# The cosine half of a transformed product in three float32r passes, in the banks of the sine half

## The chip, the cores and the metric

One NeuronCore of a Trainium2 chip runs the whole program. The metric is device time in microseconds (us): how long one execution takes. Four compute engines matter: TensorE (PE, with PEld for its weight loads) multiplies matrices into PSUM, VectorE (DVE) and ScalarE (ACT) work elementwise and read PSUM, GpSimd (POOL) works elementwise in SBUF alone and starts gathers; the SP queue starts most transfers. Each engine runs its own instructions in program order, and semaphores hold one back until what it needs from another is done.

## The reference

```python
X = np.fft.fft(x, axis=1); X = np.fft.fft(X, axis=2)    # x: (8, 3008, 256)
x = X.real.astype(np.float32).reshape(24064, 256)
h = x @ w_in                                            # w_in: (256, 2048)
g = h * np.clip(h + 3.0, 0.0, 6.0) / 6.0
out = (g @ w_out).astype(np.float32)                    # w_out: (2048, 256)
```

The real part of a two-dimensional Fourier transform of each of 8 images, and on every row of it an MLP with one hidden layer of 2048 and a hard-swish.

## The kernel before

**The transform.** The sequence of 3008 is taken as 47 x 64. `stage1` does the transform over 47 for a pair of images, `stage2` the one over 64; the transform over the 256 columns is folded into w_in, so that a row's hidden value is a cosine part plus or minus a sine part. Two output rows, k1 and N1 - k1, share both parts: h+ = c + n + s and h- = c + n - s, where n comes from one more column (`qn` times the row `WN` of folded weights). So the MLP's first product is done once for two rows, in two halves: `W1[:, 0]` with `q[:, 0]` (cosine) and `W1[:, 1]` with `q[:, 1]` (sine).

**Steps.** The program is one list of 384 steps: 4 pairs of images (p), 12 chunks of 256 columns in a pair (ck; the last of a pair has 192, or 194 in the first product), and 8 parts of the hidden layer in a chunk (fc), each of 256 hidden values, done as two blocks i of 128. t = 8 ck + fc counts the steps of a pair. The first 8 steps (0 to 7) prepare the weights beside the work, steps 8 to 21 use plain float32 products for both halves, and from `SPLIT` = 22 on the order is the one that the change touches. That loop issues, in step s:

1. `odd_half` (L642) of step s + 2: the sine half. Its six products are float32r: q and w were split by `split_q` (L605) and `split_w` (L619) into a high part, a low part and a rest, so that three passes give the exact product: the rest's pass into bank v, then high and low into bank u, on top of the cosine half that stands there. ScalarE copies v to y (L653), VectorE adds u (1 + EPS) + y in u (L655), ScalarE does the relu of it to t (L692). Between the copy and the addition come the products of a stage1 (`begin_parts`), if one is due.
2. the first n of the seven products of `mlp2` (L743) of step s: w_out, by a Strassen-like scheme of seven products for eight, three with a (the gated values) and four with sums c of a.
3. `even_half` (L627) of step s + 3: the cosine half, float32, two products (L632) into bank u, which VectorE adds to qn times `WS1` as s (L638).
4. the products of a stage2, if one is due (`middle_fns`), which ScalarE evicts to q (L529 and L490).
5. VectorE's `other_sign` (v = u - 2 (1 + EPS) s, L663), its relu, the two gates to a (L695); GpSimd's `combine` to c (L697, its adds at L709) of step s + 1, and at the head of a chunk (fc 0) the five adds of `finish` (L755) for the chunk before; VectorE's transposes of its results (L804) at fc 1 and 2.
6. the remaining products of `mlp2` of step s. At fc 7 ScalarE evicts the finished sums to e (L753).

**Banks.** PSUM has eight banks here: four of the tag acc for the output sums, and a0, a1, y0, y1. Bank u of a step is a{step % 2} and v is y{step % 2}. A stage1 or stage2 in step s takes y{(s + 3) % 2} (`bank`), a stage1 also a{(s + 3) % 2} (`other_bank`):

```python
if turn_of[0]:
    return ps_u.tile(shape, F32, tag=f"y{turn_of[0] % 2}", name=name)   # turn_of[0] = s + 3
```

A tile with a tag waits until the readers of the tag's last tile are done.

**When.** A stage2 comes at t = 3 and 7 of every 16 (fc 3 and 7), in pair 0 partly at other steps; a stage1 every ninth step of pairs 1 and 2, every sixth of pair 0 from t = 32, none in pair 3.

Of the kernel before, what the change touches and what calls it, by code (L numbers as in the profile page):

```python
# [60 lines left out]
def kernel(  # L61
# [34 lines left out]
    DH = 32  # L96
# [37 lines left out]
    C = consts.tile([P, 2, D], F32, name="C")  # L134
    W1 = consts.tile([P, 2, FF], F32, name="W1")
    WN = consts.tile([P, NFC], F32, name="WN")
    WS1 = consts.tile([P, NFC], F32, name="WS1")
    G = consts.tile([P, 7, NF, P], F32, name="G")
    half = consts.tile([P, 1], F32, name="half")
    ones = consts.tile([P, P], F32, name="ones")  # L140
# [148 lines left out]
    def stage1(pr, c):  # L289
# [16 lines left out]
        nc.scalar.copy(z[:, 1], ps[1][0:PB + PZ])  # L306
        yield
        nc.scalar.copy(z[:, 0], ps[0][0:PB + PZ])
# [57 lines left out]
    def evict_first(hb, m, ps, pt):  # L366
        k = FIRST.index(m)
        pool, tag = ((zpool, "z"), (zpool, "z"), (apool, "a"), (cpool, "c"))[k]
        z = pool.tile([P, 2, 2, D + 1], F32, tag=tag, name="z")
# [22 lines left out]
    def stage1_quarters(hb, m):  # L392
# [14 lines left out]
        nc.scalar.copy(z[:, 1], ps[1][0:PX])  # L407
        yield
        nc.scalar.copy(z[:, 0], ps[0][0:PX])
# [171 lines left out]
    def activate(ch, fc, u, v, between=None):  # L581
        of, nq, qn = ch.ck % 2 * TB, ch.nq, ch.pr.qn[ch.ck // 2]
        wn, back = (WN, 1.0) if ch.ck < 2 else (WS1, 1.0 + EPS)
        s = spool.tile([P, 2, TB], F32, tag="s", name="s")
        for i in range(2):
            f = 2 * fc + i
            nc.vector.scalar_tensor_tensor(s[:, i, 0:nq], qn[:, of:of + nq], wn[:, f:f + 1], u[:, i, 0:nq],  # L587
                                           op0=AL.mult, op1=AL.add)
# [3 lines left out]
        t = spool.tile([P, 2, 2, TB], F32, tag="t", name="t")  # L592
        ch.a[fc] = a
        nc.vector.scalar_tensor_tensor(u[:], s[:], back, v[:], op0=AL.mult, op1=AL.add)
        relu(t[:, 0], u[:], 1.0 / 6.0)
        nc.vector.scalar_tensor_tensor(v[:], s[:], -back, v[:], op0=AL.mult, op1=AL.add)
# [8 lines left out]
    def split_q(ch):  # L605

        of, nq, q = ch.ck % 2 * TB, ch.nq, ch.pr.q[ch.ck // 2][:, 1]
        k = qpool.tile([P, 3, TB], F32R, tag="k", bufs=2, name="k")
        ch.k = k
        split(k[:, 0, 0:nq], k[:, 1, 0:nq], k[:, 2, 0:nq], q[:, of:of + nq])  # L610

    def split(high, low, rest, x):
        nc.scalar.mul(high, x, 1.0 - EPS / 2.0)
        h = high.bitcast(F32)
        nc.gpsimd.tensor_tensor(low, x, h, op=AL.subtract)
        nc.scalar.mul(rest, h, EPS)
        nc.gpsimd.tensor_tensor(rest, rest, low, op=AL.subtract)

    def split_w(i):  # L619

        cs = slice(i * TB, (i + 1) * TB)
        low, rest = (spool.tile([P, TB], F32, tag="part", name="part") for j in range(2))
        split(KW[:, 0, cs], low[:], rest[:], W1[:, 1, cs])
        nc.scalar.mul(KW[:, 1, cs], low[:], 1.0 / EPS)
        nc.scalar.mul(KW[:, 2, cs], rest[:], -1.0 / EPS)

    def even_half(ch, fc, step):  # L627
        of, nq, q = ch.ck % 2 * TB, ch.nq, ch.pr.q[ch.ck // 2]
        u = ps_u.tile([P, 2, TB], F32, tag=f"a{step % 2}", name="u")
        for i in range(2):  # L630
            f = 2 * fc + i
            nc.tensor.matmul(u[:, i, 0:nq], W1[:, 0, f * P:(f + 1) * P], q[:, 0, of:of + nq],  # L632
                             start=(i == 0), stop=True, skip_group_check=True)
        qn = ch.pr.qn[ch.ck // 2]
        s = spool.tile([P, 2, TB], F32, tag="s", name="s")
        for i in range(2):
            f = 2 * fc + i
            nc.vector.scalar_tensor_tensor(s[:, i, 0:nq], qn[:, of:of + nq], WS1[:, f:f + 1], u[:, i, 0:nq],  # L638
                                           op0=AL.mult, op1=AL.add)
        ch.front[fc] = [u, s]  # L640

    def odd_half(ch, fc, step, between):  # L642
        nq, (u, s) = ch.nq, ch.front[fc]
        v = ps_u.tile([P, 2, TB], F32, tag=f"y{step % 2}", name="v")
        for j, o in ((2, v), (0, u), (1, u)):
            for i in range(2):
                fs = slice((2 * fc + i) * P, (2 * fc + i + 1) * P)
                nc.tensor.matmul(o[:, i, 0:nq], KW[:, j, fs], ch.k[:, j, 0:nq],  # L648
                                 start=(j == 2 and i == 0), stop=True, skip_group_check=True)
        y = spool.tile([P, 2, TB], F32, tag="y", bufs=1, name="y")  # L650
        t = spool.tile([P, 2, 2, TB], F32, tag="t", name="t")
# [8 lines left out]
    def other_sign(ch, fc):  # L660
        nq, (u, v, t, s) = ch.nq, ch.front[fc]
        un, vn, sn, tn = u[:, :, 0:nq], v[:, :, 0:nq], s[:, :, 0:nq], t[:, :, :, 0:nq]
        nc.vector.scalar_tensor_tensor(vn, sn, -2.0 * (1.0 + EPS), un, op0=AL.mult, op1=AL.add)  # L663
# [49 lines left out]
    def mlp2_first(ch, fc, halves=(0, 1)):  # L713
        a = ch.a[fc]
        for h in halves:
# [5 lines left out]
            if fc == NF - 1:  # L721
                if h == 0:
                    ch.r = epool.tile([P, 2, 2, TB], F32, tag="r", bufs=1, name="r")
                for m in range(2):
                    nc.scalar.mul(ch.r[:, m, h], ch.acc[h][:, m], (1 - 2 * m) / WS)

    def mlp2(ch, fc, part=None, n=3):
# [11 lines left out]
        for i, mv in order:  # L739
# [5 lines left out]
            if fc == NF - 1 and (i % 2 == 1 or i == 6):  # L745
                if i == 1:
                    ch.e = epool.tile([P, 8, TB], F32, tag="e", bufs=1, name="e")
# [7 lines left out]
    def finish(ch):  # L755
# [3 lines left out]
        w = epool.tile([P, 3, TB], F32, tag="w", bufs=1, name="w")  # L759
        r = epool.tile([P, 2, 2, TB], F32, tag="r", bufs=1, name="r")  # L760
        wn, rn = w[:, :, 0:n], r[:, :, :, 0:n]
# [676 lines left out]
```

## Time and profile before

| | us |
|---|---|
| median of 3 runs (1880.35 to 1881.13) | 1880.74 |
| the profiled execution's own time | 1880.88 |
| its span | 1879.1 |
| VectorE busy | 1421.0 (76%) |
| ScalarE busy | 949.6 (51%) |
| GpSimd busy | 1523.3 (81%) |

The granted clock of TensorE was 0.998 of full speed. In a line of the timeline stand the start and the duration in us, the engine, the line of the program, the operation, out<-in by the program's names, the shape, and how many instructions were merged; in brackets is the idle time ahead of it and what ended that. A float32 product of 256 columns is two instructions, a float32r product one. The start of a TensorE instruction can lie a little before the one ahead of it has streamed out, so lengths are read between like instructions of successive steps. Groups show the busy time and the mean of one in ns.

### The profile page before, as it was taken

The numbers are of one execution on the slowest core, as the hardware profiler recorded it, in microseconds if no ns is written. First come the engines' busy times: TensorE is split into PE (matmuls) and PEld (weight loads), VectorE is DVE, ScalarE is ACT, GpSimd is POOL, SyncE is SP. The second block draws the span as 40 slices with busy tenths as digits, with TensorE's granted clock in tenths as the row PEclk, the third lists the DMA queues.
The fourth block names the chain that finished last, engine by engine and source line by source line (L and its number), as shares of the span: only waits on it lengthen the run. The fifth ranks groups of instructions, "written<-read, shape, count | busy, mean of one in ns | idle before, by whom it ended". The sixth has DMA issues, their size and how long they took to land.

```text
span 1879.1 us, 30498 instructions
## 1 busy us (share of the span) xinstructions
PE 1861.5 (99%) x10176; PEld 1639.5 (87%) x10176; DVE 1421.0 (76%) x2756; ACT 949.6 (51%) x1647; POOL 1523.3 (81%) x1764
## 2 busy tenths in 40 slices
PE   9999999999999999999999999999999999999998
PEld 6678888888998888888998888888899898999987
DVE  8966777777777777777787777777778777777777
ACT  6545454554554554544455545445454454445443
POOL 5698999997789888898778888889777777777775
PEclk9999999999999999999999999999999999999999
DMA  7432233421112222221112221222110111101001
GB/s 267 113 100 65 63 96 82 96 56 34 49 40 60 69 69 74 53 55 44 38 49 58 58 68 51 57 64 56 48 40 21 40 28 27 42 19 40 19 22 21
DMA packets 157380, 110.42 MB, mean 59 GB/s; under 512 B 122095, under 2 KB 135898, under 8 KB 157222
## 3 DMA queue, kind: packets, MB, share of 16 engines
q1 hardware_dynamic: 144966, 71.24, 15.1%
q0 software_dynamic: 11008, 36.63, 6.7%
q8 instruction: 81, 1.33, 0.3%
q10 hardware_dynamic: 1248, 0.59, 0.1%
q14 instruction: 77, 0.63, 0.1%
HBM read 71.93 MB, written 36.79 MB: 58 GB/s over the span
## 4 chain that ended last, share of the span: by engine, by line
PE 91%; DVE 3%; POOL 2%; issue 1%; ACT 1%; DMA 1%; SPq 0%; DVEq 0%; POOLq 0%; ACTq 0%
PE acc L743 57%; PE u L632 16%; PE u L648 9%; PE v L648 4%; PE ps L526 2%; PE ps L296 1%; POOL c L709 1%; DVE a L695 1%; PE v L577 1%; PE acc L719 1%; ACT t L692 1%; PE u L577 1%; POOL xt L188 0%; DVE top L882 0%; DVE s L587 0%
## 5 line engine op out<-in xcount | busy, mean ns | idle before, releaser
L743 PE MATMUL acc<-c,G 128*128 128x256 f32 (+1 forms) x3008 | 698.6, 375 | 0.4 <-POOL c L709 0.2
L743 PEld LDWEIGHTS acc<-c,G 128*128 128x128 f32 x3008 | 564.4, 190 | 76.1 <-POOL c L709 4.5
L709 POOL TENSOR_TENSOR c<-a 128x512 f32<-128x512 f32 (+1 forms) x375 | 470.8, 1255 | 193.8 <-DVE a L695 165.6
L743 PE MATMUL acc<-a,G 128*128 128x256 f32 (+1 forms) x2256 | 599.7, 376 | 0.0
L692 ACT ACTIVATE t<-v,half 128x512 f32<-128x512 f32 (+1 forms) x384 | 261.0, 680 | 356.4 <-DVE v L663 355.0
L743 PEld LDWEIGHTS acc<-a,G 128*128 128x128 f32 x2256 | 395.2, 190 | 52.3 <-issue 14.3
L638 DVE SCALAR_TENSOR_TENSOR s<-qn,WS,u 128x256 f32<-128x256 f32 (+1 forms) x720 | 309.4, 471 | 162.2 <-PE u L632 161.2
L692 ACT ACTIVATE t<-u,half 128x512 f32<-128x512 f32 (+1 forms) x384 | 260.8, 679 | 300.1 <-DVE u L655 262.3
L655 DVE SCALAR_TENSOR_TENSOR u<-u,y 128x512 f32<-128x512 f32 (+1 forms) x360 | 245.4, 682 | 193.6 <-ACT y L653 190.5
L632 PE MATMUL u<-q,W 128*128 128x256 f32 (+1 forms) x1440 | 362.8, 374 | 0.0
L695 DVE SCALAR_TENSOR_TENSOR a<-t,v 128x512 f32<-128x512 f32 (+1 forms) x480 | 265.7, 570 | 57.3 <-ACT t L692 54.9
L632 PEld LDWEIGHTS u<-q,W 128*128 128x128 f32 x1440 | 270.5, 190 | 34.6
L653 ACT COPY y<-v 128x512 f32<-128x512 f32 (+1 forms) x360 | 208.6, 580 | 174.4 <-PE v L648 172.7
L709 POOL TENSOR_TENSOR c<-a,c 128x256 f32<-128x256 f32 (+1 forms) x375 | 269.5, 719 | 29.4
L709 POOL TENSOR_TENSOR c<-c,a 128x256 f32<-128x256 f32 (+1 forms) x375 | 269.5, 719 | 29.4
L695 DVE SCALAR_TENSOR_TENSOR a<-t,u 128x512 f32<-128x512 f32 (+2 forms) x448 | 261.0, 594 | 15.4 <-ACT t L692 15.4
L663 DVE SCALAR_TENSOR_TENSOR v<-s,u 128x512 f32<-128x512 f32 (+1 forms) x360 | 243.7, 677 | 0.9 <-ACT t L692 0.7
L648 PE MATMUL u<-k,KW 128*128 128x256 f32 (+1 forms) x1440 | 226.1, 279 | 0.0
L648 PE MATMUL v<-k,KW 128*128 128x256 f32 (+1 forms) x720 | 208.7, 371 | 0.0
L648 PEld LDWEIGHTS u<-k,KW 128*128 128x128 f32 x1440 | 193.7, 188 | 0.0
L648 PEld LDWEIGHTS v<-k,KW 128*128 128x128 f32 x720 | 136.0, 190 | 17.1
L709 POOL TENSOR_TENSOR r<-w,e 128x256 f32<-128x256 f32 (+1 forms) x92 | 88.9, 988 | 3.6
(152 smaller groups left out, 1228.9 us busy)
## 6 DMA issues: line engine op xcount, KB each, us to landing
out_dram<-o SPq DMA_DIRECT2D x744, 32.0 KB
T<-in_c_stage_dram SPq DMA_DIRECT2D x26, 512.0 KB
g<-zd SPq DMA_DIRECT2D x42, 256.0 KB
zd<-z SPq DMA_DIRECT2D x48, 192.0 KB
xt<-in_x_dram POOLq DMA_DIRECT2D x21, 256.0 KB
qn<-qd SPq DMA_DIRECT2D x16, 256.0 KB
st<-in_moe_w_out_dram POOLq DMA_DIRECT2D x7, 512.0 KB
xt<-in_x_dram POOLq DMA_DIRECT2D x17, 192.0 KB
```

The lines of the kernel that those rows point to most:

```text
L526: nc.tensor.matmul(ps[:, blk, u * P:n].rearrange("p (b k) -> p b k", b=2), g[:, kk, blk * (P + 1):blk * (P + 1) + P], T[gr][:, :, blk, kk, ...
L577: nc.tensor.matmul(ps[:, i, 0:nq], W1[r, blk, f * P:(f + 1) * P], q[r, blk, of:of + nq], start=True, stop=True)
L632: nc.tensor.matmul(u[:, i, 0:nq], W1[:, 0, f * P:(f + 1) * P], q[:, 0, of:of + nq], start=(i == 0), stop=True, skip_group_check=True)
L638: nc.vector.scalar_tensor_tensor(s[:, i, 0:nq], qn[:, of:of + nq], WS1[:, f:f + 1], u[:, i, 0:nq], op0=AL.mult, op1=AL.add)
L648: nc.tensor.matmul(o[:, i, 0:nq], KW[:, j, fs], ch.k[:, j, 0:nq], start=(j == 2 and i == 0), stop=True, skip_group_check=True)
L653: nc.scalar.copy(yn, vn)
L655: nc.vector.scalar_tensor_tensor(un, un, 1.0 + EPS, yn, op0=AL.mult, op1=AL.add)
L663: nc.vector.scalar_tensor_tensor(vn, sn, -2.0 * (1.0 + EPS), un, op0=AL.mult, op1=AL.add)
L692: nc.scalar.activation(t, h, AF.Relu, bias=half[:], scale=scale)
L695: nc.vector.scalar_tensor_tensor(dst, t, 1.0, h, op0=AL.min, op1=AL.mult)
L709: (eng or nc.gpsimd).tensor_tensor(out, in0, in1, op=AL.add)
L743: nc.tensor.matmul(ch.acc[i // 2][:, i % 2, 0:ch.n], G[:, i, fc, :], mv, start=(fc == 0 and i % 2 == 0), stop=(fc == NF - 1), skip_group_c ...
```

## The change

The cosine half gets the same three float32r passes as the sine half, into the same two banks: `even_half` of step s + 3 now opens both u and v, and `odd_half` adds the sine half to them a step later. VectorE then makes s in two stages: d = qn WN + v (two ops, as before) and s = u (1 + EPS) + d (one op more). Weights and q are split for both halves, so `split_w` and `split_q` work on twice the data, and a step earlier; `WS1` is no longer needed. Since the cosine half now takes y{(s + 3) % 2} in step s, stage2 is moved ahead of it, both evictions of a stage1 are issued together, and n is 2 in steps with a stage2 too. To make room in SBUF, `finish` and `finish_final` work in place in e, q, qn, a, c and t get one buffer fewer, and C, ones, the last two z of the start and two staging tiles move to a pool that is closed at step 7.

```diff
-    qpool = ctx.enter_context(tc.tile_pool(name="qpool", bufs=3))
+    qpool = ctx.enter_context(tc.tile_pool(name="qpool", bufs=2))
-    apool = ctx.enter_context(tc.tile_pool(name="apool", bufs=4))
-    cpool = ctx.enter_context(tc.tile_pool(name="cpool", bufs=3))
+    apool = ctx.enter_context(tc.tile_pool(name="apool", bufs=3))
+    cpool = ctx.enter_context(tc.tile_pool(name="cpool", bufs=2))
...
         nc.scalar.copy(z[:, 1], ps[1][0:PB + PZ])
+        nc.scalar.copy(z[:, 0], ps[0][0:PB + PZ])
         yield
-        nc.scalar.copy(z[:, 0], ps[0][0:PB + PZ])
...
     def split_q(ch):
-        of, nq, q = ch.ck % 2 * TB, ch.nq, ch.pr.q[ch.ck // 2][:, 1]
-        k = qpool.tile([P, 3, TB], F32R, tag="k", bufs=2, name="k")
-        ch.k = k
-        split(k[:, 0, 0:nq], k[:, 1, 0:nq], k[:, 2, 0:nq], q[:, of:of + nq])
+        of, nq, q = ch.ck % 2 * TB, ch.nq, ch.pr.q[ch.ck // 2]
+        ch.k = qpool.tile([P, 3, 2, TB], F32R, tag="k", bufs=2, name="k")
+        high, low, rest = (ch.k[:, j, :, 0:nq] for j in range(3))
+        split(high, low, rest, q[:, :, of:of + nq])
...
+    def half_products(ch, fc, blk, u, v):
+        nq = ch.nq
+        for j, o in ((2, v), (0, u), (1, u)):
+            for i in range(2):
+                fs = slice((2 * fc + i) * P, (2 * fc + i + 1) * P)
+                nc.tensor.matmul(o[:, i, 0:nq], KW[:, j, blk, fs], ch.k[:, j, blk, 0:nq], start=(blk == i == 0 and j != 1),
+                                 stop=True, skip_group_check=True)
+
     def even_half(ch, fc, step):
-        of, nq, q = ch.ck % 2 * TB, ch.nq, ch.pr.q[ch.ck // 2]
+        of, nq, qn = ch.ck % 2 * TB, ch.nq, ch.pr.qn[ch.ck // 2]
         u = ps_u.tile([P, 2, TB], F32, tag=f"a{step % 2}", name="u")
-        for i in range(2):
-            f = 2 * fc + i
-            nc.tensor.matmul(u[:, i, 0:nq], W1[:, 0, f * P:(f + 1) * P], q[:, 0, of:of + nq],
-                             start=(i == 0), stop=True, skip_group_check=True)
-        qn = ch.pr.qn[ch.ck // 2]
-        s = spool.tile([P, 2, TB], F32, tag="s", name="s")
+        v = ps_u.tile([P, 2, TB], F32, tag=f"y{step % 2}", name="v")
+        half_products(ch, fc, 0, u, v)
+        d = spool.tile([P, 2, TB], F32, tag="y", bufs=1, name="d")
         for i in range(2):
             f = 2 * fc + i
-            nc.vector.scalar_tensor_tensor(s[:, i, 0:nq], qn[:, of:of + nq], WS1[:, f:f + 1], u[:, i, 0:nq],
+            nc.vector.scalar_tensor_tensor(d[:, i, 0:nq], qn[:, of:of + nq], WN[:, f:f + 1], v[:, i, 0:nq],
                                            op0=AL.mult, op1=AL.add)
-        ch.front[fc] = [u, s]
+        s = spool.tile([P, 2, TB], F32, tag="s", name="s")
+        nc.vector.scalar_tensor_tensor(s[:, :, 0:nq], u[:, :, 0:nq], 1.0 + EPS, d[:, :, 0:nq], op0=AL.mult, op1=AL.add)
+        ch.front[fc] = [u, v, s]

     def odd_half(ch, fc, step, between):
-        nq, (u, s) = ch.nq, ch.front[fc]
-        v = ps_u.tile([P, 2, TB], F32, tag=f"y{step % 2}", name="v")
-        for j, o in ((2, v), (0, u), (1, u)):
...
+        nq, (u, v, s) = ch.nq, ch.front[fc]
+        half_products(ch, fc, 1, u, v)
...
     def finish(ch):
-        add(rn[:, 0, 0], e[:, 0], e[:, 1])
-        nc.gpsimd.tensor_tensor(wn[:, 0], e[:, 0], e[:, 5], op=AL.subtract)
-        add(wn[:, 1:3], wn[:, 0:1].to_broadcast([P, 2, n]), e[:, 4:2:-1])
-        add(rn[:, 0, 1], wn[:, 2], e[:, 6])
-        add(rn[:, 1], wn[:, 1:2].to_broadcast([P, 2, n]), e[:, 2:4])
+        add(e[:, 1], e[:, 0], e[:, 1])
+        nc.gpsimd.tensor_tensor(e[:, 0], e[:, 0], e[:, 5], op=AL.subtract)
+        add(e[:, 4:6], e[:, 0:1].to_broadcast([P, 2, n]), e[:, 4:2:-1])
+        add(e[:, 6], e[:, 5], e[:, 6])
+        add(e[:, 2:4], e[:, 4:5].to_broadcast([P, 2, n]), e[:, 2:4])
...
             for i in range(NF):
-                put(NF + 2 * i, split_w, i)
+                put(NF + 3 * i // 2, split_w, i)
...
-                n = 3 if s == SPLIT else 1 + (t in behind)
+                n = 3 if s == SPLIT else 1 + (t in behind or t in middle_fns)
...
                 if s > SPLIT:
                     mlp2(*chunk(s), 0, n)
+                run(middle_fns, t)
                 if s + 3 < len(steps):
                     even_half(*chunk(s + 3), s + 3)
-                run(middle_fns, t)
...
-            if s > SPLIT - 6 and s + 5 < len(steps) and (s + 5) % NF == 0:
-                split_q(chunk(s + 5)[0])
+            if s > SPLIT - 6 and s + 6 < len(steps) and (s + 6) % NF == 0:
+                split_q(chunk(s + 6)[0])
```

More of the change, by code (lines that the diff above doesn't have):

```diff
@@ L621, in split_w @@
         cs = slice(i * TB, (i + 1) * TB)
[L622 to L627, printed above, removed]
-        of, nq, q = ch.ck % 2 * TB, ch.nq, ch.pr.q[ch.ck // 2]
-        u = ps_u.tile([P, 2, TB], F32, tag=f"a{step % 2}", name="u")
-        for i in range(2):
-            f = 2 * fc + i
-            nc.tensor.matmul(u[:, i, 0:nq], W1[:, 0, f * P:(f + 1) * P], q[:, 0, of:of + nq],
-                             start=(i == 0), stop=True, skip_group_check=True)
-        qn = ch.pr.qn[ch.ck // 2]
-        s = spool.tile([P, 2, TB], F32, tag="s", name="s")
[L636 to L639, printed above, removed]
-        ch.front[fc] = [u, s]
-    def odd_half(ch, fc, step, between):
-        nq, (u, s) = ch.nq, ch.front[fc]
-        v = ps_u.tile([P, 2, TB], F32, tag=f"y{step % 2}", name="v")
+        high, low, rest = (KW[:, j, :, cs] for j in range(3))
+        split(high, low, rest, W1[:, :, cs])
+        nc.scalar.mul(low, low, 1.0 / EPS)
+        nc.scalar.mul(rest, rest, -1.0 / EPS)
+    def half_products(ch, fc, blk, u, v):
+        nq = ch.nq
         for j, o in ((2, v), (0, u), (1, u)):
```

80 lines of the change are left out of this document (39 added, 41 removed).

## The prediction

> **What bounds the kernel now.** I read the engine totals first, then the chain of waits that ended last.
>
> ```profile
> span 1879.1 us, 30498 instructions
> ...
> PE 1861.5 (99%) x10176; PEld 1639.5 (87%) x10176; DVE 1421.0 (76%) x2756; ACT 949.6 (51%) x1647; POOL 1523.3 (81%) x1764
> ...
> PE 91%; DVE 3%; POOL 2%; issue 1%; ACT 1%; DMA 1%; SPq 0%; DVEq 0%; POOLq 0%; ACTq 0%
> ```
>
> TensorE is busy in 99% of the span and carries 91% of the chain; nothing else decides more than 3%. Busy is no proof of peak, so I took one ordinary step from the timeline (columns: start, duration, engine, line, out<-in, count).
>
> ```profile
> 1006.94 0.58 PE L648 MATMUL v<-k,KW 128*128 128x256 f32 x2
> 1007.36 0.63 PE L648 MATMUL u<-k,KW 128*128 128x256 f32 x4
> 1007.61 0.59 ACT L653 COPY y<-v 128x512 f32<-128x512 f32 x1 [0.68 <-PE v L648]
> 1007.83 0.59 PE L743 MATMUL acc<-a,G 128*128 128x256 f32 x2
> 1008.23 0.70 DVE L655 SCALAR_TENSOR_TENSOR u<-u,y 128x512 f32<-128x512 f32 x1 [0.57 <-ACT y L653]
> 1008.26 1.02 PE L632 MATMUL u<-q,W 128*128 128x256 f32 x4
> 1008.97 0.69 ACT L692 ACTIVATE t<-u,half 128x512 f32<-128x512 f32 x1 [0.77 <-DVE u L655]
> 1009.12 1.03 PE L743 MATMUL acc<-a,G 128*128 128x256 f32 x4
> 1009.32 0.87 DVE L638 SCALAR_TENSOR_TENSOR s<-qn,WS,u 128x256 f32<-128x256 f32 x2 [0.39 <-PE u L632]
> 1010.11 0.69 DVE L663 SCALAR_TENSOR_TENSOR v<-s,u 128x512 f32<-128x512 f32 x1
> 1010.71 0.68 DVE L695 SCALAR_TENSOR_TENSOR a<-t,u 128x512 f32<-128x512 f32 x1
> 1011.52 0.58 PE L648 MATMUL v<-k,KW 128*128 128x256 f32 x2
> 1011.55 0.69 DVE L695 SCALAR_TENSOR_TENSOR a<-t,v 128x512 f32<-128x512 f32 x1 [0.17 <-ACT t L692]
> ```
>
> I write all instants below from the start of a step's sine half (1006.94 = 0). TensorE: sine half 0, one w_out product 0.89, cosine half (L632) 1.32, the other six products 2.18, next step 4.58. The float32 instructions, two to a product, cost 0.215 each (four take 9.12 - 8.26 = 0.86). Eighteen make 3.87, so the six float32r products of the sine half cost 4.58 - 3.87 = 0.71, however their stamps lie (the first is stamped some 0.19 early). VectorE begins at 1.29 with u, when ScalarE has copied y, idles until L638 at 2.38, and ends its second gate at 5.30, which is 0.72 into the next step. That rest is cover: TensorE never waits for it.
>
> Now a step with a stage2 (L526), and after it one with a stage1 (L296), from the timelines of TensorE and ScalarE.
>
> ```profile
> 1013.71 1.05 PE L526 MATMUL ps<-T,g 128*128 128x128 f32 x8
> 1014.60 1.03 PE L743 MATMUL acc<-a,G 128*128 128x256 f32 x4
> 1017.00 0.59 PE L648 MATMUL v<-k,KW 128*128 128x256 f32 x2
> 1017.99 1.09 PE L296 MATMUL ps<-y,F 47*64 47x512 f32 x8
> 1019.01 1.13 PE L743 MATMUL acc<-a,G 128*128 128x256 f32 x4
> 1022.81 0.59 PE L648 MATMUL v<-k,KW 128*128 128x256 f32 x2
> ...
> 1014.80 0.59 ACT L529 COPY q<-ps 128x512 f32<-128x512 f32 x1 [0.56 <-PE ps L526]
> 1016.00 1.84 ACT L753 ACTIVATE e<-acc 128x512 f32<-128x512 f32 x4
> 1019.14 0.59 ACT L306 COPY z<-ps 112x512 f32<-112x512 f32 x1 [0.82 <-PE ps L296]
> ```
>
> Stage2 is 0.89 of TensorE (14.60 - 13.71) and the step 5.48 (17.00 - 11.52): its eviction by ScalarE, 1.09 after the first product, costs TensorE nothing, since the next writer of that bank comes a step later. The stage1 step takes 5.81.
>
> **The change part by part.** Products: the cosine half goes from 0.86 to 0.71, a gain of 0.15, and an ordinary step to 4.43. Price bounds: 0.71, as measured between the same float32 neighbours, or six times the bare spacing of the sine half's last four (0.47 / 4 = 0.118), which is 0.71 too.
>
> VectorE: L638's two halves stay (as d), and one op of 512 from PSUM and SBUF is added, 0.60 from start to start (10.71 - 10.11), like L655. TensorE's cosine half is stamped 1.13 now (0.19 early), its last four products 1.55, the other six w_out products 2.02. VectorE's new order: u 1.29, d 1.89 (its bank is ready at 1.80, as y starts 0.25 behind the same stamp of the sine half), s 2.68, v 3.28, gate 3.88, second gate 4.72 (1.44 behind v as now, through ScalarE's relu), end 5.41. VectorE does this in 4.03, below 4.43. But the cosine half of two steps on now needs the y bank of that second gate, too. How soon TensorE follows an engine is seen in steps where it does wait:
>
> ```profile
> 1060.10 0.69 DVE L695 SCALAR_TENSOR_TENSOR a<-t,v 128x512 f32<-128x512 f32 x1 [0.17 <-ACT t L692]
> 1060.93 1.09 PE L296 MATMUL ps<-y,F 47*64 47x512 f32 x8 [0.33 <-DVE a L695]
> ...
> 1149.99 0.59 ACT L308 COPY z<-ps 112x512 f32<-112x512 f32 x1
> 1150.64 1.16 PE L526 MATMUL ps<-T,g 128*128 128x128 f32 x8
> 1151.63 0.60 PE L743 MATMUL acc<-a,G 128*128 128x256 f32 x2
> ```
>
> TensorE starts 0.14 behind VectorE's end, 0.06 behind ScalarE's, and eight products after a wait take 0.99 for 0.89, so 0.10 of refill. Gate end 5.41 + 0.14 = 5.55 against 4.43 + 1.13 = 5.56 (stamp; 1.32 by stream): an ordinary step just keeps its 0.15, with no cover left. Bounds: 0.18 kept, or 0.11 of it lost. 262 ordinary full steps: **-39** (-47 to -10).
>
> Stage2 steps. The idle bank is gone: the stage's bank y{(s+3)%2} is the one that the cosine half of step s+3 takes, so stage2 is moved ahead of it, and TensorE, in order, stands until ScalarE has emptied the bank. With two products first: stage2 1.75 to 2.64, eviction 1.75 + 1.09 = 2.84 to 3.43, cosine half 3.49: a hole of 0.85, with refill 0.95, less the 0.15: +0.80. Behind the waiting product stand the cosine half, five w_out products and the next sine half; d therefore starts at 4.1, the second gate ends at 7.62, and the cosine half after that, at 6.27 + 1.13 to 1.32, finds its bank 0.2 to 0.4 late: +0.25. How many:
>
> ```profile
> L526 PEld LDWEIGHTS ps<-T,g 128*128 128x128 f32 x320 | 41.6, 191 | 2.7 <-ACT z L308 1.0
> L296 PEld LDWEIGHTS ps<-y,F 47*64 47x64 f32 x192 | 5.0, 131 | 4.0 <-PE u L648 1.0
> ```
>
> Eight loads each: 40 stage2s, beside which the code has six stage2_half, two of them (t = 8 and 16) ahead of the split steps, so 44; and 24 stage1s, five in a step with a stage2. (The 360 split steps less 44, 19 and some 35 in last chunks are the 262.) 44 x 1.05 = 46. In 21 of them fc is 7: with n = 2 the eviction of e (four take 1.84) now stands in ScalarE's queue ahead of the bank's, +0.29: 6. In 20 fc is 3: the step before issues split_q, now of both halves:
>
> ```profile
> 1036.92 0.42 ACT L616 ACTIVATE k<-k 128x256 fp32r<-128x256 f32 x1
> 386.63 0.77 DVE L804 STREAM_TRANSPOSE o<-r 128x256 f32<-128x256 f32 x2
> ```
>
> Two ops of 0.41 fitted ahead of y; two of 0.59 end about 0.6 later than y was due, u and its relu follow, and the eviction stands behind that relu, +0.41: 8. Sum **+60**, from 30 (44 holes of 0.85, less 0.15, nothing else) to 82 (the knock-on doubled, the queue terms half as large again).
>
> Stage1 steps: stage1 can start at 1.04 behind the gate, z1 follows 1.15 behind its start (19.14 - 17.99), z0 0.60 on (now ahead of the relu of u, which moves back by as much), ends 3.38; the cosine half could have run at 3.0. Step 6.2 for 5.81, and the same knock-on: 0.65 x 19 and some 0.2 in five steps that hold a stage2 as well: **+13** (6 to 25).
>
> Transposes: two a step at fc 1 and 2 (0.77 in the row above), in the rest that s has filled. Behind the gate VectorE is free at 5.32, after them at 6.09, while u is due at 5.72: 0.4 late, and 0.7 after the second pair. The stream's 0.2 of slack takes part of it, and a stage2 step at fc 3 hides the rest; in the 24 chunks without one I take 0.35: **+8** (0 to 26).
>
> Last chunks (194 columns):
>
> ```profile
> 959.58 0.50 PE L648 MATMUL v<-k,KW 128*128 128x194 f32 x2
> 960.71 0.82 PE L632 MATMUL u<-q,W 128*128 128x194 f32 x4
> 961.37 0.81 PE L743 MATMUL acc<-a,G 128*128 128x192 f32 x4
> 963.18 0.50 PE L648 MATMUL v<-k,KW 128*128 128x194 f32 x2
> ```
>
> The four instructions take 0.66 there, 18 take 2.97, and 3.60 - 2.97 leaves 0.63 for float32r: hardly less than with 256 columns, so these 34 steps gain nothing (0.66 to 0.63), and VectorE, whose gates are seven small ops, fills all of 3.6 with the op of 388 added: 0.2 a step and the transposes in the open: **+8** (0 to 20).
>
> The Trainium skill ("TensorE: Matmul & The Clock Gate", section "LDWEIGHTS (loading the stationary operand)") says that a weight load's time goes by its 128 columns alone, columns / 1.2 ns, some 107 ns. The row agrees that width hardly counts (0.105 a product at 194 columns), but at 256 it is 0.118; at the page's 107 the half would be 0.64, the gain 0.22 a step, and the sum, by estimate, 18 us lower.
>
> GpSimd: split_q and split_w double, 0.54 more for each of their two ops. In the stretch where split_w falls GpSimd is already nearly full:
>
> ```profile
> 88.00:172.00 84.00, 80.94 (x389) 65.52 (x387) 56.66 (x103) 42.20 (x89) 75.18 (x87) 1.00 0.29 79
> 978.00:1433.00 455.00, 454.66 (x2485) 405.91 (x2484) 342.70 (x666) 230.32 (x397) 385.17 (x443) 1.00 0.22 55
> ```
>
> 75 of 84 busy (columns of the busy times: TensorE, its loads, VectorE, ScalarE, GpSimd), and eight splits add 8.7: **+4**, as half of it falls beside waits that are there already. The second row is pair 2: 385 of 455, and twelve split_q add 13; c of a step may start at 5.41 and is wanted two steps and 2.9 later, at 11.7, for 2.7 of work, so a backlog of 3 is borne: **+2** over three pairs (0 to 20 together).
>
> At nothing: buffers of q, qn, a, c, t (each is next written after, on VectorE's or TensorE's own order, its last reader is done: t0 of a step follows its u, which follows the second gate before; c's last product ends at 4.43, its next writer starts behind the gate at 5.41; without that cover GpSimd would give up at most 1 a step), finish in place (the same five ops), C, ones and z in the closing pool, WS1's op.
>
> Sum: -39 + 60 + 13 + 8 + 8 + 6 = **+56**, on the profiled execution's own 1880.88 (span and 1.8 around it; the median of the runs shown is 1880.74): **1937**.
>
> **The rivals.** (1) The bank wait is covered after all, and products alone count: 322 full steps x 0.15 = 48, **1833**. For it: ScalarE is busy half the time. Against: the eviction can't start before stage2 ends, and nothing but the cosine half is next in TensorE's order. It decides if that half's first product follows stage2 without a gap. (2) Only the bare holes: -39 + 30 + 19 x 0.4, **about 1880**, if the gate's late end is taken up by the next step. (3) VectorE's loop becomes the bound everywhere: sine half to u to second gate to the cosine half two steps on is 5.55, then 3.3 to the sine half: 8.85 for two steps, against 8.86. If d or s costs 0.3 more than its row, each ordinary step costs 0.15 and the gain is gone: +39 and the stage terms more: **about 1990**. For: no slack; against: each term is a row. (4) GpSimd becomes late for c. In pair 2 it has 4.0 of work in a mean step of 4.74, 4.15 with the change; if its idle 0.7 a step is all waits that stay, it can't go under 4.85 a step, and 0.15 over what TensorE needs in the 288 steps of pairs 0 to 2 is 43 more, **1980**. It decides where TensorE's c products wait; that the chain has TensorE at 91% and the products of c never as the profile's main wait speaks against it. (5) The change doesn't do what it says, float32r at the float32 price (the first pair's stamps lie 0.42 apart): six at 0.215 are 1.29 for 0.71, +0.58 x 322 = 187, **2124**; the step's own length speaks against it.
>
> **How the numbers follow.** Sum as worked out 0.70; (1) 0.06; (2) 0.12; (3) 0.07; (4) 0.04; (5) 0.01. The bounds of the likeliest alone give 1905 to 1970; with (4), half of (2) and half of (3) 1890 to 1985 leaves out 2 in 10. About 0.2% (4 us) is what the measurement can tell. Faster: (1) and a quarter of (2), 0.09; same 0.03; slower 0.88.
>
> **What would show it.** Ordinary steps at 4.43; stage2 steps near 6.3 to 6.7, with idle time of TensorE before the cosine half's v released by ScalarE's q copy, and in stage1 steps by z; the second gate releasing v in the steps behind these. Wrong if stage2 steps stay near 5.4, or if ordinary steps are at 4.58 and more.

## The result, and the profile after

| | before | changed | ratio |
|---|---|---|---|
| median, us (4 runs each) | 1880.84 | 2075.15 | 1.1033 (95%: 1.1014 to 1.1052) |
| lowest to highest, us | 1880.35 to 1881.13 | 2074.88 to 2075.26 | |

The change costs 194 us. The prediction, 1937 in a range from 1890 to 1985, has the direction right and the size far too small. Engine totals and the chain of waits of the changed kernel, the rows that the prediction began with:

```profile
span 2073.4 us, 32703 instructions
...
PE 1901.6 (92%) x10896; PEld 1612.6 (78%) x10896; DVE 1658.0 (80%) x3116; ACT 954.0 (46%) x1646; POOL 1584.8 (76%) x1764
...
PE 35%; DVE 33%; ACT 15%; issue 8%; POOL 7%; DVEq 1%; DMA 1%; SPq 0%; POOLq 0%; ACTq 0%
```

TensorE had 91% of the chain and has 35%; VectorE and ScalarE together have 48%. Neither of the two is busy for more than 80% of the span: the chain now passes to and fro between the three engines. The waits of TensorE that weigh most (who waits, for whom: us in total, how often, the longest):

```profile
PE v L631 <- DVE a L696: 67.5, 87, 1.2
...
PE v L631 <- ACT q L526: 47.0, 40, 1.7
```

The second row is the bank of a stage2, as forecast. The first and larger one is the bank y that the second gate of an earlier step frees. To see where it costs time I took the length of every step in both kernels, from the start of one sine half to the next (359 steps after the first), and summed the differences by kind of step; the first row is the start of the first split step, and the steps from t = 85 of a pair on count as last chunks. The other kernels of the next section stand in the same table.

```
us against before     n   forecast  changed  d_in_s  late_own  no_s_op  stage_first  best1
steps up to 21        -      +4      +17.7   +20.4    +17.2    +17.6      +16.1      +5.0
ordinary            258     -29      +70.4   +48.3    -16.5    -25.3       -5.5      -5.8
with a stage2        41     +60      +65.9   +56.1    +38.0    +37.2       +5.0      +4.9
with a stage1 only   19     +13      +18.8   +14.1     +6.1     +5.0       -2.1      -2.2
last chunks          41      +8      +22.2   +18.4     +7.7     +3.4       +5.1      +5.1
```

("Forecast" puts the prediction's transposes, +8, and its +2 of GpSimd with the ordinary steps' -39.) Ninety-nine of the missing 138 us lie in the ordinary steps. Among those of them that don't stand right behind a stage, the median step of fc 2, 5 and 7 is 4.44 to 4.48 long, as forecast, while those of fc 1 have a mean of 5.77 (4.59 before, 33 steps, +38.8), those of fc 4 of 5.55 (19 steps, +18.3) and those of fc 3 of 5.04 (18 steps, +7.7). So the products are as cheap as forecast, and what comes once a chunk is paid in full. From the timelines of ScalarE, VectorE and TensorE, over the head of one chunk:

```profile
1630.60 1.35 ACT L755 ACTIVATE e<-acc 128x512 f32<-128x512 f32 x3
1631.82 0.61 ACT L654 COPY y<-v 128x512 f32<-128x512 f32 x1
1632.46 0.70 DVE L656 SCALAR_TENSOR_TENSOR u<-u,y 128x512 f32<-128x512 f32 x1 [1.04 <-PE u L631]
...
1634.26 0.69 DVE L645 SCALAR_TENSOR_TENSOR s<-u,d 128x512 f32<-128x512 f32 x1
1634.87 0.69 DVE L664 SCALAR_TENSOR_TENSOR v<-s,u 128x512 f32<-128x512 f32 x1
1635.47 0.68 DVE L696 SCALAR_TENSOR_TENSOR a<-t,u 128x512 f32<-128x512 f32 x1
1636.31 0.69 DVE L696 SCALAR_TENSOR_TENSOR a<-t,v 128x512 f32<-128x512 f32 x1 [0.16 <-ACT t L693]
1636.92 0.69 DVE L656 SCALAR_TENSOR_TENSOR u<-u,y 128x512 f32<-128x512 f32 x1
1637.15 0.47 PE L631 MATMUL v<-k,KW 128*128 128x256 f32 x2 [0.95 <-DVE a L696]
1637.72 0.87 DVE L642 SCALAR_TENSOR_TENSOR d<-qn,WN,v 128x256 f32<-128x256 f32 x2
1638.71 0.69 DVE L645 SCALAR_TENSOR_TENSOR s<-u,d 128x512 f32<-128x512 f32 x1
...
1641.36 0.77 DVE L802 STREAM_TRANSPOSE o<-e 128x256 f32<-128x256 f32 x2
1642.05 0.67 DVE L656 SCALAR_TENSOR_TENSOR u<-u,y 128x512 f32<-128x512 f32 x1
1642.83 0.87 DVE L642 SCALAR_TENSOR_TENSOR d<-qn,WN,v 128x256 f32<-128x256 f32 x2
1643.81 0.69 DVE L645 SCALAR_TENSOR_TENSOR s<-u,d 128x512 f32<-128x512 f32 x1
...
1645.86 0.69 DVE L696 SCALAR_TENSOR_TENSOR a<-t,v 128x512 f32<-128x512 f32 x1 [0.17 <-ACT t L693]
1646.47 0.76 DVE L802 STREAM_TRANSPOSE o<-e 128x256 f32<-128x256 f32 x2
1646.70 0.47 PE L631 MATMUL v<-k,KW 128*128 128x256 f32 x2 [0.43 <-DVE a L696]
```

From s to s (34.26 to 38.71) VectorE takes 4.45 in a step without transposes, with no bracket but 0.16: it goes round without rest. Start to start: u to d 0.80, d to s 0.99, s to v 0.60, v to gate 0.60, to the second gate 0.84, to the next u 0.61; sum 4.44. The prediction had 0.60 and 0.79 for the first two and 4.03 for the sum. At 1642.83 the reason can be read off: u runs to 1642.72, d starts 0.11 after that end; d ends at 1643.70 and s starts 0.11 after. Neighbours that don't depend on each other start 0.60 apart though each lasts 0.69. The two that wait for an end are s, which reads d, and d, which writes the one buffer of the tag y that u is just reading (`bufs=1` in the diff). TensorE needs 4.44 itself, so a lateness of VectorE stays until TensorE has waited as long.

Two things make it late here. The first is ScalarE. It evicts e at the end of a chunk, and the copy y of the next step stands behind that in its queue: y starts 1.87 behind its sine half, which began at 1629.95, where a quiet step has 0.68. VectorE stands for 1.04 until y is there (u starts 0.03 behind y's end), and a step later the cosine half waits 0.95 for the second gate, at 1637.15, ahead of any transpose. That is the loss of the fc 1 steps: in the median of the 35 ordinary steps of fc 0, y starts 2.04 behind the sine half. In the kernel before it starts 1.59 behind there and costs nothing, since VectorE catches up. The second thing is the transposes. With them the round is 5.10 (38.71 to 43.81), and the waits at 1646.70 and, of 0.81, at 1652.20 follow; between them the two ops of `split_q` on ScalarE delay y once more, by which VectorE stands for 0.28. Those are the losses of fc 3 and 4. The waits at 1637.15 and 1646.70 end 0.15 behind a gate's end. This division is read from the timeline: no run moved the eviction of e or the transposes alone.

### The profile page after: what moved, and what is told of

Read it like the earlier page. It is cut to its first block, busy times and chain, and to the rows that moved or that the text cites. A ratio compares the mean times of both kernels' runs of the same rounds, so it can differ in the third digit from the quotient of the medians.

```text
span 2073.4 us, 32703 instructions
## 1 busy us (share of the span) xinstructions
PE 1901.6 (92%) x10896; PEld 1612.6 (78%) x10896; DVE 1658.0 (80%) x3116; ACT 954.0 (46%) x1646; POOL 1584.8 (76%) x1764
## 4 chain that ended last, share of the span: by engine, by line
PE 35%; DVE 33%; ACT 15%; issue 8%; POOL 7%; DVEq 1%; DMA 1%; SPq 0%; POOLq 0%; ACTq 0%
PE acc L745 20%; DVE d L642 8%; ACT t L693 7%; DVE s L645 7%; PE u L631 6%; DVE u L656 6%; DVE v L664 6%; PE v L631 6%; POOL c L710 3%; DVE a L696 3%; ACT y L654 2%; ACT e L755 2%; PE ps L293 1%; DVE o L802 1%; ACT q L526 1%
## 5 line engine op out<-in xcount | busy, mean ns | idle before, releaser
L745 PE MATMUL acc<-a,G 128*128 128x256 f32 (+1 forms) x2256 | 606.3, 379 | 2.9 <-ACT e L755 1.5
L631 PE MATMUL v<-k,KW 128*128 128x256 f32 (+1 forms) x1440 | 385.1, 349 | 125.3 <-DVE a L696 67.5
L631 PE MATMUL u<-k,KW 128*128 128x256 f32 (+1 forms) x2880 | 459.4, 282 | 0.6 <-DVE s L645 0.2
L642 DVE SCALAR_TENSOR_TENSOR d<-qn,WN,v 128x256 f32<-128x256 f32 (+1 forms) x720 | 309.9, 472 | 169.9 <-PE v L631 136.4
L631 PEld LDWEIGHTS v<-k,KW 128*128 128x128 f32 x1440 | 245.6, 189 | 238.5 <-issue 67.6
L745 PEld LDWEIGHTS acc<-a,G 128*128 128x128 f32 x2256 | 375.4, 190 | 45.2 <-issue 16.7
L631 PEld LDWEIGHTS u<-k,KW 128*128 128x128 f32 x2880 | 390.9, 189 | 4.6 <-DVE s L645 4.6
L645 DVE SCALAR_TENSOR_TENSOR s<-u,d 128x512 f32<-128x512 f32 (+1 forms) x360 | 245.0, 681 | 40.8 <-PE acc L745 0.5
L710 POOL TENSOR_TENSOR e<-e 128x512 f32<-128x512 f32 (+2 forms) x184 | 180.2, 990 | 7.2
L614 POOL TENSOR_TENSOR k<-q,k 128x512 fp32r<-128x512 f32 (+1 forms) x45 | 56.7, 1259 | 55.4 <-ACT k L609 55.2
```

The costliest lines, as they stand in the source:

```text
L631: nc.tensor.matmul(o[:, i, 0:nq], KW[:, j, blk, fs], ch.k[:, j, blk, 0:nq], start=(blk == i == 0 and j != 1), stop=True, skip_group_check= ...
L642: nc.vector.scalar_tensor_tensor(d[:, i, 0:nq], qn[:, of:of + nq], WN[:, f:f + 1], v[:, i, 0:nq], op0=AL.mult, op1=AL.add)
L645: nc.vector.scalar_tensor_tensor(s[:, :, 0:nq], u[:, :, 0:nq], 1.0 + EPS, d[:, :, 0:nq], op0=AL.mult, op1=AL.add)
L710: (eng or nc.gpsimd).tensor_tensor(out, in0, in1, op=AL.add)
L745: nc.tensor.matmul(ch.acc[i // 2][:, i % 2, 0:ch.n], G[:, i, fc, :], mv, start=(fc == 0 and i % 2 == 0), stop=(fc == NF - 1), skip_group_c ...
```

## The experiments

All times of this section are of one run (a median of five where a ratio is given); the kernel before took 1879.9 to 1882.4 beside them.

**One dependence away: d_in_s.** d is written into the tile of s, so that it doesn't share a buffer with y:

```diff
-        d = spool.tile([P, 2, TB], F32, tag="y", bufs=1, name="d")
+        d = s = spool.tile([P, 2, TB], F32, tag="s", name="s")
...
-        s = spool.tile([P, 2, TB], F32, tag="s", name="s")
```

> The changed kernel, with d written into the tile of s instead of the buffer that it shares with y. Theory A (VectorE's own order: d waits until u has ended because it takes y's buffer, s waits until d has ended; the cycle of one step is 4.46 us against TensorE's 4.43, so everything that delays VectorE is paid): u to d falls from 0.81 to 0.60 us, the cycle to 4.25, which gives 0.2 us a step back where VectorE is late, some 45 chunks x 1.6 = 70 us: 1990 to 2030. Theory B (the shared banks cost whatever VectorE does: TensorE has to wait for the second gate anyway): within 10 us of 2075.

2037.36, 38 us below the changed kernel: between the two theories, far more than B's 10 us and 7 us above A's range. A round of its VectorE:

```profile
1622.88 0.69 DVE L695 SCALAR_TENSOR_TENSOR a<-t,v 128x512 f32<-128x512 f32 x1 [0.16 <-ACT t L692]
1623.48 0.69 DVE L655 SCALAR_TENSOR_TENSOR u<-u,y 128x512 f32<-128x512 f32 x1
1623.71 0.47 PE L631 MATMUL v<-k,KW 128*128 128x256 f32 x2 [0.62 <-DVE a L695]
1624.22 0.87 DVE L642 SCALAR_TENSOR_TENSOR s<-qn,WN,v 128x256 f32<-128x256 f32 x2
1625.20 0.69 DVE L644 SCALAR_TENSOR_TENSOR s<-u,s 128x512 f32<-128x512 f32 x1
```

The addition still stands 0.98 behind d. And d, free of u's end, starts 0.74 behind u all the same: the cosine half started 0.14 behind the gate's end (1622.88 + 0.69 = 1623.57) and d 0.51 later. The shared bank has closed a loop, from the gate through TensorE to d and back to the gate.

**Both away: late_own.** As d_in_s, and the addition is issued after `other_sign`, so that VectorE's order is u, d, v, s, gate, gate:

```diff
-        nc.vector.scalar_tensor_tensor(s[:, :, 0:nq], u[:, :, 0:nq], 1.0 + EPS, d[:, :, 0:nq], op0=AL.mult, op1=AL.add)
+    def sum_cosine(ch, fc):
+        nc.vector.scalar_tensor_tensor(s[:, :, 0:nq], u[:, :, 0:nq], 1.0 + EPS, d[:, :, 0:nq], op0=AL.mult, op1=AL.add)
```

> As d_in_s, and the addition that makes s is issued behind other_sign, so that d to s and u to v are no longer neighbours that wait for each other, and the relu of v starts 1 us earlier. Theory A: cycle 0.6 + 0.8 + 4 x 0.6 = 3.8 us, well below 4.43; ordinary steps 4.43 to 4.5, what stays are the holes behind stage1 and stage2 and the start: 1910 to 1950. Theory B: above 2030.

1932.58, as theory A had it: the same instructions in another order, with d in the tile of s, take 105 us less than d_in_s and 143 less than the changed kernel.

```profile
1541.03 0.59 PE L631 MATMUL v<-k,KW 128*128 128x256 f32 x2
1542.33 0.70 DVE L660 SCALAR_TENSOR_TENSOR u<-u,y 128x512 f32<-128x512 f32 x1 [0.38 <-ACT y L658]
1542.93 0.86 DVE L642 SCALAR_TENSOR_TENSOR s<-qn,WN,v 128x256 f32<-128x256 f32 x2
1543.78 0.70 DVE L668 SCALAR_TENSOR_TENSOR v<-s,u 128x512 f32<-128x512 f32 x1
1544.38 0.68 DVE L649 SCALAR_TENSOR_TENSOR s<-u,s 128x512 f32<-128x512 f32 x1
1544.99 0.68 DVE L700 SCALAR_TENSOR_TENSOR a<-t,u 128x512 f32<-128x512 f32 x1
1545.47 0.59 PE L631 MATMUL v<-k,KW 128*128 128x256 f32 x2
1545.58 0.68 DVE L700 SCALAR_TENSOR_TENSOR a<-t,v 128x512 f32<-128x512 f32 x1
```

Every start is 0.59 to 0.61 behind the one ahead of it, d's two ops 0.85; with 0.60 to the next u the round is 3.85, and u has a bracket again (0.38 for ScalarE's y). Of the 0.59 saved, 0.20 is u to d, 0.14 is behind d, and 0.25 lies between the gates: the addition now fills the time in which ScalarE makes the second relu. TensorE's step is 4.44 (41.03 to 45.47). Its waits, beside the changed kernel's 67.5 and 47.0:

```profile
PE v L631 <- ACT q L526: 30.7, 40, 0.9
...
PE v L631 <- DVE a L700: 2.2, 6, 1.2
```

**The addition left out: no_s_op.** As d_in_s, without the addition.

> The changed kernel without the addition u (1 + EPS) + d: s is d alone, so the high and low parts of the cosine half are left out of h-. Banks, products, order and evictions stay. Theory A: VectorE's cycle 3.5 us, ordinary steps at TensorE's 4.43, the stage holes and the start stay: 1915 to 1950. Theory B: above 2030.

1918.62. It takes an op from every round, where late_own only moves it, and gains 14 us more; 143 of the 157 are thus the order of that op and the buffer, not its work. Both runs lie in theory A's ranges.

**One more op on VectorE before the change: extra_op.** To the kernel before, an op of the same size that changes nothing, dependent on s, is added to every step:

```diff
+        nc.vector.scalar_tensor_tensor(s[:, :, 0:nq], u[:, :, 0:nq], 0.0, s[:, :, 0:nq], op0=AL.mult, op1=AL.add)
```

> The kernel before, with one more VectorE op of 512 a step that reads bank u and s and writes s unchanged, waiting for s as in the changed kernel; no float32r cosine half, no shared bank. Theory A (the load hurts only where the bank is wanted two steps on, and in the kernel before VectorE has 0.7 us of cover behind the second gate and 0.3 ahead of s): 1881 to 1905. Theory C (VectorE's load alone is the cause, banks don't matter): 245 us more work in VectorE shows as 100 us or more, above 1980.

1920.42, between the two ranges. The ordinary steps of fc 3, 4, 6 and 7 stay within 0.03 us of their lengths, so the work as such doesn't lengthen a step; but 32 of the 38 us fall on steps of fc 0 (+10.4), on stage1s (+9.9 and +3.7) and on the last chunks (+8.1; the +3.7 are stage1s in steps with a stage2). At fc 0 TensorE waits for ScalarE's eviction of e (14.1 us of its weight loads, 1.5 before), which stands behind a relu that comes later now, and at a stage1 for the second gate (12.9 us, 0.7 before). I had taken the cover of an ordinary step for that of all.

**The stages: stage_first.** late_own, with a stage2's products right behind the sine half, in front of the w_out products, so that ScalarE empties the bank while TensorE has four w_out products to do:

```diff
+    def begin_stages(t):
+        if t not in behind:
+            run(middle_fns, t)
+        return begin_parts(t)
...
-                n = 3 if s == SPLIT else 1 + (t in behind or t in middle_fns)
+                n = 3 if s == SPLIT or t in behind else 1 + (t in middle_fns)
...
-                    odd_half(*chunk(s + 2), s + 2, lambda: begin_parts(t))
+                    odd_half(*chunk(s + 2), s + 2, lambda: begin_stages(t))
...
-                run(middle_fns, t)
+                if t in behind:
+                    run(middle_fns, t)
```

> late_own with the products of a stage2 issued right behind the sine half, its eviction ahead of the relu of u in ScalarE's order, and the two w_out products between it and the cosine half; with three of them behind a stage1. Theory H (the hole is the time from stage2's end to the end of its eviction, about 0.85 us, that nothing is issued into): the eviction ends at 2.63 and TensorE gets there at 2.64, stage2 steps fall from 6.3 to 6.5 to 5.4, 44 x 0.9 = 40 us: 1888 to 1900. Rival R (the bank's chain only moves: the later relu and gates make the next cosine half wait): no more than 15 us, above 1915.

1898.79, as theory H had it. First the stage2 step of the changed kernel, at fc 7, then that of this one:

```profile
1623.43 0.59 PE L631 MATMUL v<-k,KW 128*128 128x256 f32 x2
...
1625.19 1.05 PE L523 MATMUL ps<-T,g 128*128 128x128 f32 x8
...
1626.05 0.59 ACT L755 ACTIVATE e<-acc 128x512 f32<-128x512 f32 x1
...
1626.52 0.59 ACT L526 COPY q<-ps 128x512 f32<-128x512 f32 x1
...
1627.16 0.51 PE L631 MATMUL v<-k,KW 128*128 128x256 f32 x2 [0.92 <-ACT q L526]
```

```profile
1471.94 0.59 PE L631 MATMUL v<-k,KW 128*128 128x256 f32 x2
...
1472.84 1.13 PE L523 MATMUL ps<-T,g 128*128 128x128 f32 x8
1473.80 1.03 PE L749 MATMUL acc<-a,G 128*128 128x256 f32 x4
1474.00 0.59 ACT L526 COPY q<-ps 128x512 f32<-128x512 f32 x1 [0.67 <-PE ps L523]
...
1474.64 0.50 PE L631 MATMUL v<-k,KW 128*128 128x256 f32 x2
```

In the first, TensorE stands for 0.92; the eviction is issued behind that of e, and the next cosine half follows its end, 1627.11, by 0.05. In the second the w_out products run meanwhile, and there is no bracket. The stage2 steps lose 5 us against before, not 38.

**The stages alone: stage_only.** The same order on the changed kernel, whose VectorE is left as it is.

> The changed kernel with the stage order of stage_first alone: VectorE's order stays as the change has it. In late_own that order was worth 1932.6 - 1898.8 = 34 us. If VectorE is the bound of the changed kernel (theory A), part of a stage hole is time in which VectorE catches up what it is late, and closing the hole gives back less: 5 to 25 us, 2050 to 2070. If the terms simply add up (rival): 34, 2038 to 2044.

2042.65: 32.5 us gained, beside the 33.8 from late_own to stage_first. The rival of plain addition is right. I had thought that VectorE's lateness would swallow most of the gain. The terms are alike one by one, too: the stage2 steps give back 34 us here and 33 there, the stage1 steps 8 in both, and the ordinary steps take 11 more in both. Why they do is not shown.

**The start: split_late and scale_apart.** split_late spaces the eight `split_w` two steps apart, as before; scale_apart also takes ScalarE's scaling of the parts out of it, as `scale_w`, and issues that three steps later (the last line of the diff).

```diff
-                put(NF + 3 * i // 2, split_w, i)
+                put(NF + 2 * i, split_w, i)
+                put(NF + 2 * i + 3, scale_w, i)
```

> The changed kernel with split_w at every second step, as before, instead of two in three. The split steps begin 17.7 us later than before. Theory S (ScalarE, in order, stands behind GpSimd in every split_w and the relus of the step behind it): the same eight waits, spread over more steps, 8 to 15 us of the 17.7 stay: 2063 to 2073. Theory G (GpSimd's 8.7 us of work more in a stretch where it is nearly full): spread to t = 22, 2 to 8 us stay: 2057 to 2065.

> As split_late, and ScalarE scales low and rest three steps behind the split, so that it no longer waits for GpSimd in the same step. Theory S: the start is within 4 us of the kernel before, 10 us or more below split_late. Theory G: within 3 us of split_late.

2070.24 and 2063.23; the first split step comes 12.3 and 4.5 later than before, not 17.7. In the waits of the changed kernel and of the kernel before stand, one row from each:

```profile
ACT KW L623 <- POOL KW L616: 30.3, 8, 6.6
```

```profile
ACT KW L624 <- POOL part L615: 17.9, 8, 4.5
```

Eight times ScalarE stands up to 6.6 us for GpSimd's subtraction, with the copies and relus of the steps behind it in its queue. In split_late the row is 28.8, in scale_apart it is gone. GpSimd's work is the same in all of them, so 13 of the 17.7 us were this wait and the closer spacing, as theory S has it in kind; scale_apart misses its two bounds, 4.5 for 4 left and 7 for 10 below split_late. How the 13 divide is less clear, since split_late's first `split_w` begins 1.9 late already (94.64 for 92.75), behind a stretch of half clock from 16.9 to 23.7 us, ahead of anything that its edit touches. With that taken off, spacing and wait are worth 7 and 5, else 5 and 8.

Some of the 17.7 is such a clock as well. In the changed kernel the granted clock of TensorE was 0.50 from 110.7 to 114.1 us, 1.1 behind a stand of 2.73, and from 131.2 to 138.0, begun in one of 3.55; the kernel before has no such stretch until 1873 us.

```profile
132.13 2.07 PE L574 MATMUL v<-q,W 127*128 127x256 f32 x4 [3.55 <-DVE a L696]
```

The same four instructions take 1.03 at 117.35. TensorE was busy for 3.4 and 5.9 us of the two stretches; half of that, 4.6, is an estimate of what they cost. Scale_apart has one of 3.4 there. Three more of 3.4 in the split steps (at 670.5, 1356.5 and 1605.7) are, in the same way, some 5 us of the 194.

**All three together: best1.** late_own, stage_first and scale_apart, in five runs.

> late_own, stage_first and scale_apart together. If the three terms are apart: 1932 - 40 - 15 = 1877, 1870 to 1885.

1886.97, ratio 1.0036 (1.0020 to 1.0052): just slower than before, two us above the expectation. Its waits show what is left:

```profile
PEld acc L753 <- POOL c L718: 33.7, 48, 3.1
```

Now GpSimd is last: TensorE waits for c, 33.7 us, where the kernel before had 4.5 in that row. The steps of fc 4, behind `split_q`, are 4.92 in the mean at a median of 4.44 (without those right behind a stage, as in all such means here).

**GpSimd relieved: q_on_dve and best2.** best1, with the two subtractions of `split_q` on VectorE; best2 those of `split_w` too.

> best1 with the two subtractions of split_q on VectorE, one step later, instead of GpSimd. In best1 TensorE waits 33 us for GpSimd's c products, nearly all in pairs 0 to 2. If GpSimd's fill is that wait's cause, 45 x 2 x 1.26 us less there takes away half of it or more, and VectorE has 0.6 us a step for the 1.2: 1865 to 1875. If not, or if VectorE pays as much: 1883 and above.

> q_on_dve, and split_w's subtractions on VectorE too. GpSimd's c waits at the start (10 us) shrink: 2 to 6 us below q_on_dve, 1860 to 1872, faster than the kernel before.

1946.53, and 1947.36 (1.0354, from 1.0340 to 1.0368): 60 us lost where I expected a gain. The timeline, and the groups of the two subtractions:

```profile
1547.38 0.68 DVE L612 TENSOR_TENSOR k<-q,k 128x512 fp32r<-128x512 f32 x1
1547.61 1.60 POOL L725 TENSOR_TENSOR c<-a 128x512 f32<-128x512 f32 x1 [1.39 <-PE u L642]
1548.10 1.65 DVE L613 TENSOR_TENSOR k<-k 128x512 fp32r<-128x512 f32 x1
...
1549.68 0.69 DVE L671 SCALAR_TENSOR_TENSOR u<-u,y 128x512 f32<-128x512 f32 x1
```

```profile
L613 DVE TENSOR_TENSOR k<-k 128x512 fp32r<-128x512 f32 x41 | 62.5, 1525 | 1.4
...
L612 DVE TENSOR_TENSOR k<-q,k 128x512 fp32r<-128x512 f32 x41 | 37.2, 908 | 0.0
```

A subtraction that takes 0.68 undisturbed takes 1.65 beside GpSimd's addition, which takes 1.60 itself for 1.28. The u behind it starts 2.3 after the first subtraction, and the steps of fc 5 go from 4.53 in best1 to 5.80. The weight loads' wait for c does fall, from 33.7 to 19.0, but TensorE now waits for s (29.1 us, 40 times), so that this doesn't show what GpSimd's relief alone is worth. best2's further step changes nothing beyond that.

**The splits a step earlier: best3.** best1 with `split_q` for step s + 5, and `split_w` and the scaling two steps later, in five runs.

> best1 with split_q one step later (three steps behind finish in GpSimd's order instead of two) and split_w from t = 10 to 24. GpSimd does as much as in best1, but less of it in a row. If best1's 33 us of waits for c come from work in a row: a third of them goes, and with the start 1870 to 1880, below the kernel before. If from the total alone: 1883 to 1890.

1889.70, ratio 1.0047 (1.0033 to 1.0061). The start is within 0.7 us of before, yet TensorE's waits for c still sum to 28.9: they lose a seventh and not a third, and the time lies where the total alone was to put it. The loss has moved along with `split_q`, from fc 4 (now 4.47) to fc 5 (4.74), and fc 2 has gone from 4.61 to 4.73. No version that I ran beats the kernel before; best1 comes nearest.

## Why the prediction was wrong

**The step that failed** is "VectorE does this in 4.03, below 4.43". The durations came from rows and the order was right, but the spacings were those of neighbours that don't depend on each other. Two of the new neighbours do: u to d 0.80 for 0.60, d to s 0.99 for 0.79. With that the round is 4.44, TensorE's own step, and 0.4 of cover that the sum relied on was never there. late_own, whose neighbours are independent, has a round of 3.85, and its ordinary steps come out 16.5 below before, where the changed kernel's are 70.4 above. The trace of before held the sign. In the early steps of the plain products one op follows the s that it reads:

```profile
L594 DVE SCALAR_TENSOR_TENSOR u<-s,v 128x512 f32<-128x512 f32 x24 | 16.7, 697 | 2.7
```

24 ops with 2.7 of idle time ahead, 0.11 each, on an engine that else starts ops before the last one ends. I did not ask which neighbours depend on each other; and in the list of buffers "at nothing" the tag that d shares with y was not looked at, which alone is worth 38 us (d_in_s).

**What hung on it.** With a round as long as the step nothing is made up. The eviction of e was priced in the 21 stage2 steps of fc 7 alone, +6, and everywhere else at nothing without a word; behind it the fc 1 steps cost 39. The transposes were put at +8, since "the stream's 0.2 of slack takes part of it"; with `split_q`, whose ops on ScalarE were priced in stage2 steps alone, too, they cost 26 at fc 3 and 4. The last chunks, +22 for +8, fall with the same cause (+7.7 in late_own). The rival that described this, the third, had the mechanism and its condition ("If d or s costs 0.3 more than its row"; together they cost 0.40 more), but too small a price, 1990: it let each ordinary step lose its 0.15 and left the periodic work where it was. Its loop can be seen where nothing periodic falls: from 1655.38 to 1664.54 two steps of the changed kernel take 9.15, for its 8.85.

**The price of the products** was right: 4.44 a step in late_own and no_s_op for a forecast of 4.43. TensorE starts 0.15 behind VectorE's end and 0.05 behind ScalarE's, for 0.14 and 0.06.

**Stage2** was right in kind and nearly in size, +65.9 for +60, but not term by term. With VectorE at ease (late_own) the step is 6.27 at fc 3, a hole of 0.79 for 0.80, and 6.52 at fc 7, 0.25 more with e in the queue for 0.29. In the changed kernel fc 7 is 6.52 all the same, so the +0.25 of knock-on isn't there, while fc 3 is 7.47: there the lateness of VectorE adds to the hole. The bare holes, with e, are thus 38 us for 41, and 28 is the lateness, for 19; that the sum comes close is in part luck. stage_first shows that the hole isn't inherent in the shared bank but in the place of the products.

**Stage1** cost 18.8 for 13, 6.1 in late_own: the place was right, the knock-on larger.

**The start** was mis-sized, +17.7 for +4. I had counted GpSimd's work and not who stands behind it: wider spacing and ScalarE's waiting ops moved back give 13 of it back together, and the half clock behind TensorE's stands was no term at all.

**The other rivals.** (1) fell: TensorE waits in all 40 stage2s. (2) fell, as nothing takes up the gate's late end. (4), GpSimd late for c, was not yet visible in the changed kernel and became the last bound in best1 once the rest was out of the way. (5) fell with the step of 4.44.

Why best1's remaining ordinary steps give 6 us and not 39 is read from its waits for c and the steps where they fall; no run took GpSimd's load away without a cost elsewhere, so that share isn't shown by an experiment.

## What to carry to other kernels

Before you add up an engine's round from start-to-start rows, mark which neighbours depend on each other, through a value or through a shared buffer, and put the end of the one ahead there; then look for independent work to stand between them. Compare the round, with all that comes only once in a while, to the step of the engine that bounds: where the two are equal, every rare op is paid in full, also one on another engine that the round waits for. A bank that gets a second user turns the lateness of its old reader into a wait of the new writer, so the place of the writer in its engine's order is part of the change.

## What the runs showed of the hardware

Two neighbours on VectorE start 0.60 apart at 512 columns while each lasts 0.69; if the second depends on the first, it starts 0.11 after that one's end (0.80 and 0.98 in place of 0.60 and 0.85 in the rows above). The Trainium skill ("VectorE: DVE Perf Modes", section "The DRAIN you can't avoid") says that a pipeline flush stands behind every op, that one which is not held starts earlier, and that a semaphore after each of eight copies cost nothing extra. The overlap agrees with the second of these. The last is about copies with and without a semaphore; a neighbour that needs the result of the one ahead is another case, and here it costs: the order alone was worth 105 us between d_in_s and late_own, a part of that by the relu which the moved op covers.

In q_on_dve VectorE's subtractions, which read two operands from SBUF, and GpSimd's additions slowed each other: 1525 ns in the mean for 0.68 us, and 1.60 us for 1.28 on GpSimd. Of the 82 subtractions of 512 columns the 25 that started while no addition ran on GpSimd took 0.68 to 0.69, the other 57 up to 2.61. The other ops of VectorE's round take one of the two from PSUM and show no such stretch in the rows above. The Trainium skill ("SBUF — State Buffer", section "Who interferes with whom") says that such an op shares its second read with GpSimd, as an exclusive lock by which the later one waits for the whole of the earlier; the long ops of q_on_dve agree.
